# First batch in a fixed order, and another order of products and sums, in a spectral filter with a gated feed-forward block

## The chip, the core and the metric

The kernel runs on one core of one Trainium2 chip. The metric is the time on the device in microseconds (us), from the first instruction to the last, as the median of several runs. A profile is one execution taken by the hardware profiler; its times are counted from the start of that execution.

A core has a matrix engine (TensorE, PE in the profile; its weight loads have a row of their own, PEld), a vector engine (VectorE, DVE), an engine for functions of one operand (ScalarE, ACT), a general engine (GpSimd, POOL) and a queue engine (SyncE, SP). Each takes its own instructions in the order of the program and waits on semaphores for the others. TensorE writes to PSUM alone, where the kernel keeps one bank for the spectral part and seven for the rest. GpSimd does not read PSUM here.

## The reference, cut to what matters

```python
# x: 8 x 3008 x 256, filt_r and filt_i: 1505 x 256, w_gate and w_val: 256 x 1536, w_out: 1536 x 256
X = np.fft.rfft(x, axis=1)
Y = X * (filt_r + 1j * filt_i)[None, :, :]
y = np.fft.irfft(Y, n=x.shape[1], axis=1).astype(np.float32)
t = y.reshape(24064, 256)
g = t @ w_gate
silu = g * (1.0 / (1.0 + np.exp(-g)))
out = (silu * (t @ w_val) @ w_out).astype(np.float32)
```

The three weights arrive as 64-bit floats; the kernel reads each as two 32-bit words and rounds it on the chip.

## The kernel before

The transform of 3008 = 47 x 64 points runs in three stages of matmuls with tables: stage 1 (47 points) writes to a DRAM buffer d1, stage 2 reads it back transposed, multiplies by a table, by the filter and by a table again, and writes d2, stage 3 reads d2 and yields the sequence. Batch 0 passes stages 1 and 2 in a prologue; those of each later batch run beside the feed-forward products of the batch before it.

The feed-forward part works on chunks of 376 tokens, with a third of the hidden units at a time: 8 batches x 4 chunks x 3 thirds = 96 steps. The products are not plain block products: four blocks of tokens and weights are combined in sums and differences, so that 26 products P, Q, A, B, E (two matmuls each, for the gate and for the value) do the work of 32, and seven products W (six matmuls each) do that of eight in the second matmul. The order of everything in a step is one list of tokens. A token with a prime belongs to the step before:

```python
SCHEDULE = """
P3 x1.o' h23' g03' v12' Q0 x2.o' h03' Q2 x3.o' f0 x4.o' t0.0 x03 f2 x5.o' S01' x23 Q1 t0.1 P0 f1
P2 S00' c0 W1 s13 g0 t0.2 D01 c2 S11' y02 g2 h0 P1 o1 S10' Q3 c1 y01 A13 g1 x01 g3 S21' h1 e01
t1.0 y12 m13 s01 E01 S20' t1.1 A01 D02 W6 m01 t1.2 D12 l01 B13 u01 o6 B01 v01 g13 W7 S31' h13 g01
n3' t0.3 s02 h01 t2.0 S30' s12 t1.3 o7 A02 e13 t2.1 A12 h2 W4 m02 e23 m12 s03 E13 o4 E23 l13 B12
t2.2 u13 A03 g12 v13 t2.3 t3.0 e03 m03 h3 h12 B02 t3.1 E03 W5 g02 s23 l03 e02 h02 u03 A23 v03 t3.2
o5 E02 m23 t3.3 W2 l23 n2 l02 u23 v23 u02 t4.0 o2 e12 W3 v02 t4.1 E12 o3 B23 t4.2 l12 B03 x0.o
t4.3 n1 g23 u12
""".split()
BLOCKS = (3, 0, 2, 1)
```

P, Q, A, B, E are products; f, c, s, x, y, e, m, l prepare and combine their operands in PSUM; g, u are the gate's function, h, v the product with the value; D, S, n are sums of operands on GpSimd; W an output product, o its sum; t3.1 is the second slot for a piece of spectral work. What the tokens do:

```python
        def step(self, op):
            kind, at = op[0], op[1:]
            ij = [int(c) for c in at]
            i, j = ij[0], ij[-1]
            t, v, act = self.tiles, nc.vector, nc.scalar
            diagonal = len(ij) == 1
            if kind in "PQ":
                first = (kind == "P") == (i == 3)
                if first:
                    self.bank(f"k{i}")
                self.product(op, f"k{i}", first)
            elif kind == "f":
                pin(act.mul(self.small(f"f{i}", f"f{i}", 1), t[f"k{i}"], -1.0))
            elif kind == "D":
                pin(sub(nc.gpsimd, self.small(f"D{at}", "D", 2), t[f"f{i}"], t[f"f{j}"]))
            elif kind == "c":
                pin(act.copy(out=self.small(f"c{i}", f"c{i}", 1), in_=t[f"k{i}"]))
            elif kind == "x" or kind == "s" and at not in VIA_SBUF[0]:
                dst = self.small(f"x{at}", "x", 3) if kind == "x" else self.bank(f"a{at}")
                pin(v.scalar_tensor_tensor(
                    out=dst, in0=t[f"k{j}"], scalar=-1.0, in1=t[f"f{i}" if j == 3 else f"D{at}"],
                    op0=ALU.mult, op1=ALU.add))
            elif kind == "s":
                pin(act.copy(out=self.bank(f"a{at}"), in_=t[f"x{at}"]))
            elif kind == "y" or kind == "e" and at not in VIA_SBUF[1]:
                dst = self.small(f"y{at}", "y", 2) if kind == "y" else self.bank(f"e{at}")
                pin(negated_sum(dst, t[f"k{j}"], t[f"c{i}"]))
            elif kind == "e":
                pin(act.copy(out=self.bank(f"e{at}"), in_=t[f"y{at}"]))
            elif kind in "AB":
                self.product(op, f"a{at}", False)
            elif kind == "m":
                pin(act.copy(out=self.small(f"m{at}", "m", 3), in_=t[f"a{at}"]))
            elif kind == "E":
                self.product(op, f"e{at}", False)
            elif kind == "l":
                pin(sub(v, t[f"e{at}"], t[f"e{at}"], t[f"m{at}"]))
            elif kind in "gu":
                ps = t[f"k{i}" if diagonal else f"{'a' if kind == 'g' else 'e'}{at}"]
                pin(act.activation(out=self.small(op, "g", 3, 1)[:, 0], in_=ps[:, 1], func=AF.Silu))
            elif kind in "hv":
                ps = t[f"k{i}" if diagonal else f"{'a' if kind == 'h' else 'e'}{at}"]
                g = t[("g" if kind == "h" else "u") + at][:, 0]
                dst = self.place(i, j) if kind == "h" else self.place(j, i)
                pin(v.tensor_tensor(out=dst, in0=ps[:, 0], in1=g, op=ALU.mult))
            elif kind == "S":
                h = self.hs[j]
                dst, a, b, f = ((4, 1, 2, add), (7, 4, 0, sub), (5, 0, 1, sub), (6, 3, 7, sub))[i]
                pin(f(nc.gpsimd, h[:, dst], h[:, a], h[:, b]))
            elif kind == "n":
                if self.following:
                    combine_sequence(self.following(), i)
```

Rounding half a weight (36 such halves), and the combinations of one third's weights:

```python
    def round_half(i):
        # ... (raw words in raw; tiles pw and w from pools of two buffers)
        pin(v.tensor_scalar(out=man, in0=high, scalar1=0xFFFFF, scalar2=None,
                            op0=ALU.bitwise_and))
        pin(v.tensor_scalar(out=pw, in0=high, scalar1=20, scalar2=0x7FF,
                            op0=ALU.logical_shift_right, op1=ALU.bitwise_and))
        pin(nc.scalar.activation(out=w, in_=man, func=AF.Copy, scale=2.0 ** -20, bias=1.0))
        pin(nc.scalar.activation(out=pw, in_=pw, func=AF.Relu, bias=off_t))

        load_weights(i + NRAW - 1)
        yield
        pin(v.tensor_scalar(out=pw, in0=pw, scalar1=255.0, scalar2=2.0 ** 23,
                            op0=ALU.min, op1=ALU.mult))
        pin(v.scalar_tensor_tensor(out=pw.rearrange(flat), in0=raw.rearrange(flat2)[:, :, 1],
                                   scalar=0x80000000, in1=pw.rearrange(flat),
                                   op0=ALU.bitwise_and, op1=ALU.bitwise_or))
        pin(v.scalar_tensor_tensor(out=w.rearrange(flat), in0=raw.rearrange(flat2)[:, :, 0],
                                   scalar=2.0 ** -52, in1=w.rearrange(flat),
                                   op0=ALU.mult, op1=ALU.add))
        e = nc.gpsimd
        pf = pw.bitcast(FP32)
        if use == "proj":
            j, l = at
            dst = wo_t[:, j]
            pin(e.tensor_tensor(out=dst[:, ts(l, 2), :], in0=w, in1=pf, op=ALU.mult))
        # ... (four more sums for a w_out half; for a w_gate or w_val half two products and up to two sums, all on GpSimd)
    def round_next():

        i = rounding[0]
        rounding[0] += 1
        for h in halves[i:i + 1] + (halves[i - 1:i] if i else []):
            next(h, None)

    def combine_weights(g, i, j):

        d = j - i
        wt_f = weights_of(0, 0, g).rearrange("p s z f -> p s (z f)")
        m = wt_f[:, SLOT[f"A{i}{j}"]]
        ui, uj, yi, yj = [wt_f[:, SLOT[f"{p}{q}"]] for p in "PQ" for q in (i, j)]
        if d == 1:
            pin(negated_sum(m, ui, uj))
        else:
            pin(add(nc.vector, m, ui, uj))
            pin(nc.vector.tensor_scalar(out=m, in0=m, scalar1=-1.0 / d, scalar2=None, op0=ALU.mult))
        pin(sub(nc.vector, wt_f[:, SLOT[f"B{i}{j}"]], yi, m))
        pin(add(nc.gpsimd, wt_f[:, SLOT[f"E{i}{j}"]], yj, m))

    # when they run in batch 0: step -> token -> what follows it (r: one round_next)
    eight = {t: "r" for t in ("P3", "Q1", "P1", "E01", "W6", "W7", "A12", "E23")}
    pairs = {"E13": [(0, 3)], "B12": [(2, 3), (0, 2)], "E03": [(0, 1), (1, 2)], "A23": [(1, 3)],
             "B03": [0, 1, 2, 3]}
    PREPARE = {0: eight | pairs | {t: "r" for t in ("A01", "E02", "W3", "B23")},
               1: eight | pairs,
               2: {t: "r" for t in ("P3", "Q1", "P0", "P2")},
               3: {t: "r" for t in ("P3", "Q1", "P0", "P2")}}
```

Batch 0's prologue and the parts of it that the change touches:

```python
        def stage1(self, u):

            p1 = spool0 if self.b == 0 and u % 2 else t1pool
            t1 = p1.tile([NK, NV, C], FP32, name=f"t1_{self.b}_{u}", tag="t1", bufs=2)
            ps = self.bank(f"pa_{self.b}_{u}")
            self.pinned(nc.tensor.matmul(out=ps[0:NK], lhsT=wf_t, rhs=self.x.pop(u),
                                         start=True, stop=True))
            if self.b:
                self.load_x(u + 3)
            yield
            copy = nc.scalar.copy if self.b else nc.vector.tensor_copy
            self.pinned(copy(out=t1, in_=ps[0:NK]))
            queue = nc.scalar if self.b else nc.gpsimd
            self.pinned(queue.dma_start(out=self.d1_rows[:, ts(u, NV), :], in_=t1))
        # ... stage2a(u): two matmuls into ps, then
            lo, hi = slice(0, 64), slice(64, 128)
            v = nc.vector
            if self.b:
                fi = f[hi, 1]
                pin(v.tensor_tensor(out=pt, in0=ps, in1=f[:, 0], op=ALU.mult))
            else:
                fi = f[hi]
                for h in (lo, hi):
                    v.tensor_tensor(out=pt[h], in0=ps[h], in1=f[lo], op=ALU.mult)
            self.pinned(v.scalar_tensor_tensor(out=qt[lo], in0=ps[hi], scalar=-1.0, in1=fi,
                                               op0=ALU.mult, op1=ALU.mult))
            yield
            self.pinned(v.tensor_tensor(out=qt[hi], in0=ps[lo], in1=fi, op=ALU.mult))
            yield
            self.pinned(add(nc.gpsimd, pt, pt, qt))
        # ... stage2b(u): two matmuls of pt, a ScalarE copy to g, two stores to d2 from ScalarE's queue
        for i in range(4):
            spec.load_x(i)
        spec.load_tables()
        for i in range(NRAW - 1):
            load_weights(i)
        nc.sync.dma_start(out=wi_t, in_=wi_dram.ap())
        def run(piece):
            for _ in piece:
                pass

        for u in range(N_ONE):
            run(spec.stage1(u))
        for _ in range(4):
            round_next()
        lag = 3
        for u in range(N_TWO + lag):
            if u < N_TWO:
                run(spec.stage2a(u))
            if u >= lag:
                run(spec.stage2b(u - lag))
    for i in range(2):
        spec.load_t4(0, i)
    following = Spectral(1)
    for u in range(3):
        following.load_x(u)
    for _ in range(5):
        round_next()
    for i, j in PAIRS:
        combine_weights(0, i, j)
    warm()
    for step in range(4):
        run(spec.stage3(0, step))
    for d in (2, 3, 1):
        combine_sequence(spec.y[0], d)
```

At the end the list is passed once more for the last step's output products, and then its o tokens with a prime: the last sums, and six stores on GpSimd's queue.

## Time and profile before

| | us |
|---|---|
| median of 3 runs | 3137.53 (3137.41 to 3138.02) |
| span of the profiled execution | 3139.4 |
| TensorE busy | 2989.7 (95%) |
| TensorE weight loads busy | 2831.6 (90%) |
| VectorE busy | 1974.2 (63%) |
| GpSimd busy | 1585.3 (50%) |
| ScalarE busy | 1513.4 (48%) |
| mean granted TensorE clock | 0.982 |

The page of a profile has one row per engine in 40 equal slices, each digit being the busy share in tenths, and a row with the clock that the throttle granted to TensorE. A view by stretches gives the same for any cuts, in microseconds. The timeline prints merged instructions in order of time; what stands in brackets behind one is the idle time of its engine before it and who ended it ("0.92 <-ACT we L634": 0.92 us, ended by ScalarE's instruction of line 634 that writes tile we). The table of waits sums these. A line number of the kernel names a group of instructions: L268 to L282 are the rounding, L453, L479, L504 and L525 the matmuls of stages 1, 2 (twice) and 3, L603 the products and L679 the output products. A tile's name is the program's own: wk, wa and we are the banks of the P and Q, A and B, and E products. An fp32 matmul is recorded as two instructions of TensorE.

### The profile page before, as it was taken

What the parts mean: (1) busy time and instruction counts of PE and PEld (TensorE: products, weight loads), DVE (VectorE), ACT (ScalarE), POOL (GpSimd) and SP (SyncE); (2) the same over time, 40 slices, a digit from 0 to 9 for tenths busy, and PEclk for the clock granted to TensorE, in tenths of its full rate; (3) what the DMA queues carried; (4) which work ended last, traced back from release to release, by engine and by line L of the source; (5) the groups of instructions that cost most, each with busy time, mean ns of one, the idle gap of its engine ahead of it and who ended that gap; (6) DMA issues with size and microseconds to landing.
All of it is one profiled execution on the core that took longest, in us unless ns stands there. A gap on an engine that the chain in (4) does not pass through costs nothing.

```text
span 3139.4 us, 57065 instructions
## 1 busy us (share of the span) xinstructions
PE 2989.7 (95%) x20124; PEld 2831.6 (90%) x20124; DVE 1974.2 (63%) x4446; ACT 1513.4 (48%) x3898; POOL 1585.3 (50%) x1778
## 2 busy tenths in 40 slices
PE   5578999999999999999999999999999999999997
PEld 2467999999999999999999999999999999999997
DVE  4576666557665666656665576656666566666664
ACT  1344445554455544554455545555445544455542
POOL 2555545455554556445454555445554545555543
PEclk9778999999999999999999999999999999999998
DMA  8435655557655556456554566555664565544441
GB/s 238 142 126 175 210 184 176 176 177 224 185 165 174 191 187 201 159 174 203 189 183 163 186 211 191 161 179 187 203 195 154 179 200 182 188 148 141 141 133 51
DMA packets 210503, 551.72 MB, mean 176 GB/s; under 512 B 32502, under 2 KB 105462, under 8 KB 209362
## 3 DMA queue, kind: packets, MB, share of 16 engines
q1 hardware_dynamic: 150572, 462.06, 46.3%
q10 hardware_dynamic: 49408, 58.22, 6.4%
q0 software_dynamic: 10240, 27.80, 2.5%
q8 instruction: 161, 2.64, 0.3%
q14 instruction: 122, 1.00, 0.1%
HBM read 462.76 MB, written 85.20 MB: 175 GB/s over the span
## 4 chain that ended last, share of the span: by engine, by line
PE 80%; ACT 5%; DVE 3%; POOL 2%; issue 1%; DMA 1%; ACTq 1%; POOLq 0%; DVEq 0%
PE wa L603 21%; PE wA L679 14%; PE wk L603 13%; PE we L603 11%; PE wG L679 8%; PE wF L679 4%; PE pd L525 3%; PE pa L453 3%; PE pc L504 2%; PE pb L479 2%; DVE y L218 1%; ACT g L645 1%; ACT c L622 1%; ACTq L513 1%; DMA out_dram<-o 1%
## 5 line engine op out<-in xcount | busy, mean ns | idle before, releaser
L603 PE MATMUL wa<-y_t,wt_t 128*128 128x188 f32 x4560 | 867.1, 327 | 12.2 <-POOL w L302 5.3
L603 PEld LDWEIGHTS wa<-y_t,wt_t 128*128 128x128 f32 x4560 | 739.8, 191 | 53.7 <-issue 19.3
L679 PE MATMUL wA<-wo_t,h 128*128 128x128 f32 x4608 | 587.5, 278 | 17.4 <-POOL wo_t L290 11.2
L679 PEld LDWEIGHTS wA<-wo_t,h 128*128 128x128 f32 x4608 | 569.3, 194 | 24.1 <-POOL wo_t L290 11.6
L214 POOL TENSOR_TENSOR h<-h 128x376 f32<-128x376 f32 x576 | 552.5, 984 | 0.0
L603 PE MATMUL wk<-y,wt_t 128*128 128x188 f32 x3040 | 536.0, 325 | 14.5 <-ACT f L618 14.5
L214 DVE TENSOR_TENSOR we<-we,m 128x376 f32<-128x376 f32 x576 | 311.3, 556 | 375.8 <-ACT m L638 177.1
L603 PEld LDWEIGHTS wk<-y,wt_t 128*128 128x128 f32 x3040 | 494.4, 192 | 31.6 <-ACT f L618 15.4
L603 PE MATMUL we<-y_t,wt_t 128*128 128x188 f32 x2280 | 454.4, 328 | 32.2 <-ACT we L634 29.0
L603 PEld LDWEIGHTS we<-y_t,wt_t 128*128 128x128 f32 x2280 | 366.3, 191 | 71.2 <-ACT we L634 37.1
L638 ACT COPY m<-wa 128x376 f32<-128x376 f32 x576 | 270.3, 476 | 280.5 <-PE wa L603 246.1
L211 POOL TENSOR_TENSOR h<-h 128x376 f32<-128x376 f32 x192 | 185.0, 987 | 430.2 <-DVE h L650 429.7
L645 ACT ACTIVATE g<-wa 128x188 f32<-128x188 f32 x576 | 188.6, 328 | 425.6 <-PE wa L603 267.4
L214 POOL TENSOR_TENSOR D<-f,f 128x376 f32<-128x376 f32 x288 | 280.3, 987 | 72.2 <-ACT f L618 72.1
L645 ACT ACTIVATE u<-we 128x188 f32<-128x188 f32 x576 | 185.0, 326 | 247.6 <-DVE we L214 239.2
L679 PEld LDWEIGHTS wG<-wo_t,h 128*128 128x128 f32 x2304 | 283.9, 193 | 12.5 <-issue 10.7
L679 PE MATMUL wG<-wo_t,h 128*128 128x128 f32 x2304 | 291.3, 277 | 0.0
L211 POOL TENSOR_TENSOR lent<-lent 128x512 f32<-128x512 f32 (+2 forms) x94 | 116.2, 1237 | 326.3 <-DVE lent L495 304.8
L668 POOL DMA_DIRECT2D out_dram<-o x192 | 110.8, 582 | 315.5 <-DVE o L211 313.4
L650 DVE TENSOR_TENSOR h<-wa,g 128x188 f32<-128x188 f32 x576 | 201.6, 350 | 83.9 <-ACT g L645 79.0
L650 DVE TENSOR_TENSOR h<-we,u 128x188 f32<-128x188 f32 x576 | 201.7, 350 | 78.2 <-ACT u L645 68.3
L218 DVE SCALAR_TENSOR_TENSOR y<-wk,c 128x376 f32<-128x376 f32 x288 | 157.2, 546 | 99.6 <-ACT c L622 98.3
(108 smaller groups left out, 3777.2 us busy)
## 6 DMA issues: line engine op xcount, KB each, us to landing
wt_t<-w_all SPq DMA_DIRECT2D x186, 896.0 KB
wt_t<-w_all SPq DMA_DIRECT2D x186, 768.0 KB
t<-d SPq DMA_DIRECT2D x64, 384.0 KB
lent<-d SPq DMA_DIRECT2D x180, 128.0 KB
d<-lent ACTq DMA_DIRECT2D x180, 128.0 KB
d<-t ACTq DMA_DIRECT2D x112, 192.0 KB
lent<-de_tbl SPq DMA_DIRECT2D x84, 256.0 KB
lent<-in_filt_r_dram SPq DMA_DIRECT2D x336, 64.0 KB
```

Of the source, the lines that this page charges most:

```text
L211: return eng.tensor_tensor(out=dst, in0=a, in1=b, op=ALU.add)
L214: return eng.tensor_tensor(out=dst, in0=a, in1=b, op=ALU.subtract)
L218: return nc.vector.scalar_tensor_tensor(out=dst, in0=a, scalar=-1.0, in1=b, op0=ALU.mult, op1=ALU.subtract)
L453: self.pinned(nc.tensor.matmul(out=ps[0:NK], lhsT=wf_t, rhs=self.x.pop(u), start=True, stop=True))
L479: self.pinned(nc.tensor.matmul(out=ps[:, i, :], lhsT=self.tb[u][:, i, 0, :], rhs=t2[:, i, :], start=True, stop=True))
L525: self.pinned(nc.tensor.matmul(out=psv[:, n, :], lhsT=self.t4[k, i][:, n, ts(cb, 128)], rhs=wi_t, start=True, stop=True))
L603: pin(nc.tensor.matmul(out=ps[:, z], lhsT=self.wt[:, SLOT[p], z], rhs=rhs, start=start and z == 0, stop=True, skip_group_check=True))
L638: pin(act.copy(out=self.small(f"m{at}", "m", 3), in_=t[f"a{at}"]))
L645: pin(act.activation(out=self.small(op, "g", 3, 1)[:, 0], in_=ps[:, 1], func=AF.Silu))
L650: pin(v.tensor_tensor(out=dst, in0=ps[:, 0], in1=g, op=ALU.mult))
L668: pin(nc.gpsimd.dma_start(out=rows[(TOK[t] + skip) // NH:(TOK[t] + 128) // NH, ts(2 * k + i, NH), :], in_=outs[b, k][i][skip:128, t, :]))
L679: pin(nc.tensor.matmul(out=self.tiles[at][:, t, :], lhsT=self.hs[i][:, HID[p], t0:t0 + 128], rhs=wo_t[:, JB * q + i, WO[p], :], start=star ...
```

## The change

It has five parts.

1. Batch 0's prologue is pinned to the order in which the program is written (later batches were already). Eight half weights are loaded in it ahead of the last third of the stage tables, into the room of that third, and their rounding and the first third's combinations run before stage 2; eight further rounding calls run before stage 3. What is left for batch 0's steps is spread anew. Stage 1's copies move from VectorE to ScalarE.
2. In batch 0's stage 2, one product of 128 partitions takes the place of two of 64; ScalarE copies the filter's real part to both halves for it. The d2 stores move from ScalarE's queue to SyncE's and GpSimd's, and stage 3's first results use the seven banks. The warming matmuls before stage 3 become 28, of which the 14 new ones have 512 columns.
3. The list of tokens has another order; the blocks' order changes with it, the tiles of y and m get one buffer more, those of h lose one of eight parts, since the sum S2 overwrites an operand.
4. In the weights' combinations the B part moves from VectorE to GpSimd.
5. At the end the sums S are split over VectorE and GpSimd, the output products of the last step run in an order of their own, and its stores go out on three queues.

The diff, cut to its core:

```diff
 SCHEDULE = """
-P3 x1.o' h23' g03' v12' Q0 x2.o' h03' Q2 x3.o' f0 x4.o' t0.0 x03 f2 x5.o' S01' x23 Q1 t0.1 P0 f1
-P2 S00' c0 W1 s13 g0 t0.2 D01 c2 S11' y02 g2 h0 P1 o1 S10' Q3 c1 y01 A13 g1 x01 g3 S21' h1 e01
-t1.0 y12 m13 s01 E01 S20' t1.1 A01 D02 W6 m01 t1.2 D12 l01 B13 u01 o6 B01 v01 g13 W7 S31' h13 g01
-n3' t0.3 s02 h01 t2.0 S30' s12 t1.3 o7 A02 e13 t2.1 A12 h2 W4 m02 e23 m12 s03 E13 o4 E23 l13 B12
-t2.2 u13 A03 g12 v13 t2.3 t3.0 e03 m03 h3 h12 B02 t3.1 E03 W5 g02 s23 l03 e02 h02 u03 A23 v03 t3.2
-o5 E02 m23 t3.3 W2 l23 n2 l02 u23 v23 u02 t4.0 o2 e12 W3 v02 t4.1 E12 o3 B23 t4.2 l12 B03 x0.o
-t4.3 n1 g23 u12
+Q0 o3' t4.2' W2 f0 S00' S01' x0.o' t0.0 x1.o' Q1 t0.1 x2.o' P3 x3.o' f1 t4.3' W1 x4.o' S10' x03 S11'
+s13 x5.o' P1 o1 t0.2 P0 o2 c1 D01 A13 g1 c0 S20' Q2 S21' g0 y01 m13 t1.0 h0 f2 s01 W6 t1.1 h1 x23
+D02 P2 o6 D12 A01 c2 B13 g2 n3' m01 t0.3 S30' t1.2 x02 W7 S31' g13 y12 y02 B01 h13 o7 t1.3 t2.0 s02
+s12 g01 h2 Q3 t2.1 h01 e12 A02 y23 W4 e02 y03 m02 g3 A12 o4 t2.2 E12 m12 B02 t2.3 l12 E02 u12 e13
+g02 t3.0 h3 s23 l02 B12 v12 E13 t3.1 h02 u02 A23 n2 l13 g12 v02 W5 s03 e23 h12 e01 m23 A03 o5 u13
+E23 t3.2 m03 v13 E01 l23 e03 t3.3 t4.0 l01 u23 B23 v23 u01 t4.1 E03 n1 v01 g23 B03 l03 W3 h23 g03
+u03 h03 v03
 """.split()
 KS = (-1, 0, 1, 2)
-BLOCKS = (3, 0, 2, 1)
+
+LAST = "W1 o1 W2 o2 W6 o6 W5 o5 W3 o3 x0.o x1.o x2.o W7 o7 W4 o4 x3.o x4.o x5.o".split()
+BLOCKS = (0, 1, 3, 2)
 # ...
-        pin(sub(nc.vector, wt_f[:, SLOT[f"B{i}{j}"]], yi, m))
+        pin(sub(nc.gpsimd, wt_f[:, SLOT[f"B{i}{j}"]], yi, m))
 # ...
-    eight = ...   # (the old PREPARE, as above)
+    PREPARE = {(0, "B03"): [("k", 1, p) for p in range(4)], (1, "B03"): [("k", 2, 0)],
+               (2, "A01"): [("k", 2, p) for p in (1, 2, 3)]}
+    for step, tokens in ((0, "Q0 P3 P0 Q2 A01 B01"), (1, "Q0 P3 P1 A13 P2 B13 Q3 A12 B02 B12"),
+                         (2, "A13 P2 B01 A02")):
+        for token in tokens.split():
+            PREPARE.setdefault((step, token), []).append("r")
+    for g, pairs in ((1, "0Q313 0A0201 0A1202 0B0212 0B1223 0A2303"),
+                     (2, "1A0213 1E1201 1E0202 2Q112 2P123 2Q203")):
+        for p in pairs.split():
+            PREPARE.setdefault((int(p[0]), p[1:-2]), []).insert(0, ("c", g, int(p[-2]), int(p[-1])))
 # ...
-        for n in (TQ, 2 * TQ):
+        for n in (512, 512, TQ, 2 * TQ):
 # ...
-            copy = nc.scalar.copy if self.b else nc.vector.tensor_copy
-            self.pinned(copy(out=t1, in_=ps[0:NK]))
+            pin(nc.scalar.copy(out=t1, in_=ps[0:NK]))
 # ...
-            if self.b:
-                fi = f[hi, 1]
-                pin(v.tensor_tensor(out=pt, in0=ps, in1=f[:, 0], op=ALU.mult))
-            else:
-                fi = f[hi]
-                for h in (lo, hi):
-                    v.tensor_tensor(out=pt[h], in0=ps[h], in1=f[lo], op=ALU.mult)
-            self.pinned(v.scalar_tensor_tensor(out=qt[lo], in0=ps[hi], scalar=-1.0, in1=fi,
-                                               op0=ALU.mult, op1=ALU.mult))
+            fr, fi = (f[:, 0], f[hi, 1]) if self.b else (self.real.pop(u), f[hi])
+            pin(v.tensor_tensor(out=pt, in0=ps, in1=fr, op=ALU.mult))
 # ...
+        def real_part(self, u):
+
+            if u < N_TWO:
+                self.real[u] = early("fr", u)
+                for h in (slice(0, 64), slice(64, 128)):
+                    pin(nc.scalar.copy(out=self.real[u][h], in_=self.f[u][0:64]))
 # ...
+                queue = nc.scalar if self.b else (nc.sync, nc.gpsimd)[p]
 # ...
-                dst, a, b, f = ((4, 1, 2, add), (7, 4, 0, sub), (5, 0, 1, sub), (6, 3, 7, sub))[i]
-                pin(f(nc.gpsimd, h[:, dst], h[:, a], h[:, b]))
+                dst, a, b, f = ((4, 1, 2, add), (6, 4, 0, sub), (1, 0, 1, sub), (5, 3, 6, sub))[i]
+                pin(f(eng or nc.gpsimd, h[:, dst], h[:, a], h[:, b]))
 # ...
+                    queue = (nc.sync, nc.scalar, nc.gpsimd)[t] if last else nc.gpsimd
 # ...
+        for i, n in enumerate((0, 2, 2, 4)):
             spec.load_x(i)
-        spec.load_tables()
-        for i in range(NRAW - 1):
 # ...
+            if u in (7, 8, 10, 11, 13, 14, 15):
+                round_next()
+        for _ in range(2):
             round_next()
+        for u in range(3):
+            spec.load_two(u)
+        spec.load_tables(2)
+        for i, j in PAIRS:
+            combine_weights(0, i, j)
+        for u in range(3):
+            spec.real_part(u)
 # ...
+    warm()
+    for _ in range(8):
         round_next()
-    for i, j in PAIRS:
-        combine_weights(0, i, j)
-    warm()
     for step in range(4):
         run(spec.stage3(0, step))
-    for d in (2, 3, 1):
-        combine_sequence(spec.y[0], d)
+    for d in (2, 1, 3):
+        combine_sequence(spec.y[0], d, nc.vector if d == 1 else nc.gpsimd)
 # ...
+                        g0.step(op, nc.vector if ghost and op[0] == "S" and op[2] == "1" else None)
 # ...
-    for token in SCHEDULE:
-        if token.endswith("'") and (token[0] == "o" or ".o" in token):
-            older.project(token.rstrip("'"))
+    for op in LAST:
+        older.project(op, True)
```

## The prediction

> **What bounds the kernel now.** I read the page first. Part 1 has TensorE busy for 95% of the span; part 2 shows where it is not:
>
> ```profile
> PE   5578999999999999999999999999999999999997
> PEclk9778999999999999999999999999999999999998
> ```
>
> From the fifth slice on (one slice is 78 us) TensorE is full and its clock is full. The loss lies in the first four slices and the last. So I cut the trace into stretches: start to the end of the first stage's matmuls (37 us), the wait behind it (to 56.2), the second stage (to 95.7), warming and third stage (to 115), then four work steps of batch 0, from one first wk product to the next; then one step far inside, and the tail. The columns are length, then busy us (and instructions) of each engine, granted clock, DMA share and GB/s:
>
> ```profile
> 37.00:56.20 19.20, 0.03 (x1) 0.06 (x1) 8.04 (x21) 3.34 (x8) 7.25 (x15) 1.00 0.78 236
> 56.20:95.70 39.50, 27.48 (x97) 19.68 (x98) 35.58 (x53) 6.45 (x11) 15.83 (x14) 0.96 0.54 143
> 95.70:115.00 19.30, 14.32 (x61) 11.99 (x60) 9.31 (x26) 7.82 (x18) 7.45 (x15) 0.77 0.70 197
> 115.00:181.10 66.10, 34.57 (x129) 30.47 (x128) 40.67 (x113) 24.69 (x59) 36.96 (x53) 0.68 0.49 168
> 181.10:235.10 54.00, 39.87 (x211) 36.64 (x211) 41.98 (x103) 24.22 (x62) 29.29 (x46) 0.81 0.26 81
> 235.10:275.30 40.20, 33.81 (x200) 30.70 (x199) 23.05 (x60) 19.20 (x50) 21.89 (x28) 0.87 0.64 220
> 275.30:313.60 38.30, 32.89 (x201) 29.78 (x200) 25.53 (x60) 17.90 (x48) 21.38 (x30) 0.91 0.41 132
> 2852.40:2879.60 27.20, 26.28 (x190) 25.89 (x189) 17.78 (x41) 13.70 (x39) 18.04 (x19) 1.00 0.38 125
> 3103.10:3139.40 36.30, 19.04 (x122) 18.10 (x120) 8.08 (x17) 2.02 (x7) 11.00 (x14) 0.73 0.07 21
> ```
>
> The reader is to see: work steps 0 to 3 take 66.1, 54.0, 40.2 and 38.3 us; later ones 27.2 to 31. In steps 0 and 1 VectorE carries 41 to 42 us, over twice the 17.8 us of a plain step, because the weights' rounding runs there. TensorE waits for it at 0.68 of its clock. In the second stage VectorE is busy 35.6 of 39.5 us: it is the bound there.
>
> Inside, the matmuls come at a fixed pace. The timeline shows 0.64 us for one product (two matmuls) and 1.34 us for one output product (six). A plain step has 26 products and 7 output products: 26 x 0.64 + 7 x 1.34 = 26.0 us. It takes 27.2, so 1.2 us is bubble. Most is one wait, once a step:
>
> ```profile
> 2865.18 0.87 PE L603 MATMUL we<-y_t,wt_t 128*128 128x188 f32 x4 [0.92 <-ACT we L634]
> ```
>
> E01 waits for ScalarE's copy into its bank. In batch 1 (368.4 us between equal places of two batches) 7.4 us are bubble: 12 steps of 26.0 make 312, the spectral matmuls at their median start-to-start paces (32 x 0.433, 96 x 0.216, 128 x 0.112 us) 49; so 0.62 us a step on the mean.
>
> **What the Trainium skill says.** "TensorE: Matmul & The Clock Gate", What's actually happening: an idle window of about 3.4 us halves the clock, a busy one restores it. The trace agrees in steps 0 to 3 (0.68 to 0.91), but not wholly: the first stage's 94x512 matmuls pass at 0.85 us for half a product, and at 0.43 later, though TensorE is busy throughout. "SBUF — State Buffer", Who interferes with whom: a VectorE instruction with two SBUF inputs shares a read interface with GpSimd. It fits that the 128x256 subtractions of the weights take 0.41 us at best and 0.96 at most. "DMA: Bandwidth & Descriptors", Issuing engines are not separate DMA queues: more queues save only issue time; no run here isolates that yet, and I count the three store queues so.
>
> **The change, part by part.**
>
> 1. *Up to the second stage.* Eight half weights are loaded and nine rounding calls run while VectorE was nearly idle (8.0 of the 19.2 us, 8.3 of the first 37). One call costs VectorE 0.28 + 0.28 + 0.28 + 0.42 + 0.41 = 1.7 us at the shortest durations, ScalarE 0.40 + 0.49, GpSimd about 3 x 0.455. A third of the tables (2 MB) loads after the second stage's first data rather than before; two MB of weights come in earlier. The wait at 37 to 56 ran at 236 GB/s with the queue full, so bytes decide it: I count about 1 MB less ahead, 4 us, and start the second stage at 52.
>
> 2. *Second stage.* The two 64-partition products by the real filter (0.69 us each) become one of 128 (0.68); ScalarE copies make its operand. VectorE per unit: 0.68 + 0.69 + 0.68 = 2.06 us for 2.75; the units came every 2.85 us and should come every 2.1. ScalarE gets 0.59 + two 64x512 copies, some 0.5 each by the 0.59 of its 128x512 copy; GpSimd 1.26 + a store's issue of 0.53. All are under 2.1. But the weights' combinations (12 GpSimd sums of 0.84) stand before GpSimd's first sum, to about 58 us; I add 3. VectorE ends at 52 + 3 + 25 = 80, against 92.3.
>
> 3. *To the first product.* Eight rounding calls now stand between, for five. Calls follow one another at the pace of the loop VectorE, ScalarE, VectorE, GpSimd, for the tiles w and pw have two buffers: before, the L268 operations began at 96.5, 101.4, 106.0, 108.5, so 4.0 apart with a wait for loads among them. I take 3.5: 28 us, to 108; the third stage's copies and sums add 4. First product at 112 (before: 115.0). The warming matmuls grow from 8.5 us to about 20 by their columns (a row of 512 is 0.43 us at full clock, twice for a product), hidden in those 28.
>
> 4. *Steps 0 to 3.* They keep 20 rounding calls out of 28: six, ten, four, none, for twelve, eight, four, four. The B combinations go to GpSimd, so a combination costs VectorE 0.4 to 0.7 us. Step 0: plain VectorE work without output sums 17.8 - 7 x 0.55 = 14 us, 6 x 1.7 = 10, combinations 3.4, third stage 1, together 28, and 9 of waits in the in-order queue, half of what it had (66.1 - 40.7 = 25): 37. Step 1: 17.8 + 17 + 2 + 1 = 38, and 5: 43. Step 2: 17.8 + 6.8 + 2 = 27, under TensorE's own 30.5: 33. Step 3: 30.5. Sum 143.5 against 198.6, so 55 us, and 3 from the earlier beginning: **58 us**.
>
> 5. *Inside.* In the new order E01 stands third from last among the E products, some 15 us after its operand is made; the first E, E12, has one output product and A12 (2.0 us) behind its last producer. By the same prefix sums the tightest pair is A23 behind its copy s23, some 0.5 us. I take a quarter of a us off each of about 92 steps: **23 us**, out of the 57 (0.62 each) that are there.
>
> 6. *The end.* Last products end at 3107.9. GpSimd's eight sums run to 3115.6 and hold TensorE; six stores are issued at 3127.1 for 3.45 us, on one queue. Now the sums are split over two engines: 4 x (0.98 + 0.55) = 6.1 us if they exclude each other, under the first three output products. Seven output products are 9.4 us, the last sum 0.8, one issue 0.6; behind its last issue GpSimd's queue took 8 us to close, and I keep that. About 21 from the last product for 31.5: **10 us**.
>
> Sum 58 + 23 + 10 = 91; I take 87 for what in-order queues add that I don't see, so 3050.
>
> **Rivals.** (a) *A new wait in the ordered start.* Stores of the first stage stand behind GpSimd's rounding, ScalarE's copies behind rounding halves that wait for VectorE; if a call costs 4 us there, stage one ends 10 us later and the rounding is not hidden. For it: the 3.5 us loop. Against: 19 us of idle follow anyway. It would make 3070. (b) *DMA becomes the bound in the second stage*: 512 KB a unit in 2.1 us is 250 GB/s, plus 2 MB of tables, against 271 reached in the first 37 us. Then units stay at 2.6 and 6 us are lost: 3056. (c) *The new order brings as many bubbles as it removes*: VectorE's share rises to about 0.8 where a second stage runs beside products, and an in-order queue delays a copy. Then nothing comes from part 5: 3073. (d) *All bubbles vanish and step 1 stays near TensorE's pace*: 3010.
>
> **Range and chances.** (a) and (c) together give 3093, (d) 3010. The 2% line is at about 3075; only a failure of part 4 by half or two rivals at once reaches it. Faster by over 2%: 0.77; within 2%: 0.20; slower: 0.03, if the new order costs over 1.5 us in each step.
>
> **What would show it.** Right: L268 instructions from the first 25 us; second-stage units every 2.1 us; first wk near 112; steps 0 to 3 of about 37, 43, 33, 31 us with VectorE over 0.8 busy in the first two; plain steps of 26.5 to 27.0 with no 0.9 us wait of E01; last store issued some 13 us after the last product. Wrong: GpSimd idle behind VectorE in the first stage with a later second stage, plain steps at 27.2 or more, or a new releaser above 10 us in the table of waits inside.

## The result, and the profile after

The changed kernel takes **3044.4 us** (3043.3 to 3047.2), the kernel before 3137.5 us in the same series: a ratio of 0.9706, 95% interval 0.9689 to 0.9723. Predicted were 3050. The total is right, but two of its three terms are not: the start gave little more than half of what was counted, and the inside more than twice as much.

First the two rows of the page of the kernel after that answer to those shown of before, TensorE's busy share and its clock in 40 slices of 76 us:

```profile
PE   5779999999999999999999999999999999999998
PEclk9889999999999999999999999999999999999999
```

One slice fewer is short of full: TensorE is full from the fourth on. Then its table by stretches, cut at the same places of the program as before: the wait ahead of the second stage (from 37 us in both), the second stage, the calls and the third stage, steps 0 to 3, a plain step, and the end from the last F output product. That product stands elsewhere in the new order, so the ends are compared in the second table and not by these last rows. Columns: stretch, length, busy us (instructions) of TensorE, weight loads, VectorE, ScalarE, GpSimd, then clock, DMA share, GB/s.

```profile
37.00:55.50 18.50, 0.01 (x1) 0.04 (x1) 11.15 (x27) 8.64 (x18) 12.99 (x25) 1.00 0.75 199
55.50:92.00 36.50, 26.08 (x93) 20.15 (x94) 28.82 (x43) 17.56 (x29) 25.05 (x28) 0.86 0.73 196
92.00:121.10 29.10, 23.14 (x92) 14.41 (x91) 11.81 (x39) 7.93 (x18) 12.74 (x28) 0.93 0.86 259
121.10:162.60 41.50, 30.52 (x126) 26.26 (x127) 35.45 (x76) 23.40 (x58) 27.56 (x39) 0.76 0.44 141
162.60:212.50 49.90, 38.71 (x212) 34.86 (x211) 40.45 (x97) 26.02 (x66) 30.21 (x48) 0.83 0.34 108
212.50:249.10 36.60, 32.72 (x200) 29.08 (x200) 30.08 (x63) 18.92 (x49) 28.61 (x36) 0.95 0.73 242
249.10:279.40 30.30, 30.30 (x201) 27.76 (x200) 17.34 (x41) 16.26 (x43) 12.24 (x15) 1.00 0.51 161
2859.30:2885.20 25.90, 25.90 (x190) 25.90 (x189) 17.20 (x42) 13.41 (x38) 12.22 (x16) 1.00 0.41 132
3019.20:3043.30 24.10, 8.93 (x74) 8.22 (x72) 7.43 (x10) 0.00 (x0) 4.44 (x5) 0.84 0.11 33
```

The first wk product comes at 121.1 us, later than before (115.0). Steps 0 to 3 take 41.5, 49.9, 36.6 and 30.3 us; in the first two VectorE is busy 0.85 and 0.81 of the time. The plain step is 25.90 us with TensorE busy for 25.90 of them: no bubble is left in it. From this come the three terms (before minus after, in the two profiles):

| part | before | after | gained | predicted |
|---|---|---|---|---|
| to the start of step 4 | 313.6 | 279.4 | 34.2 | 58 |
| start of step 4 to start of step 95 (91 steps) | 2766.9 | 2712.5 | 54.4 | 23 |
| start of step 95 to the end | 58.9 | 51.4 | 7.5 | 10 |
| span | 3139.4 | 3043.3 | 96.1 | 91 |

The expectations below have 55 and 6.7 us for the second and third gain, from a start of step 95 in the kernel before that was read 0.8 us late.

### The profile page after: what moved, and what is told of

Read it like the earlier page. It is cut to its first block, busy times and chain, and to the rows that moved or that the text cites. A ratio compares the mean times of both kernels' runs of the same rounds, so it can differ in the third digit from the quotient of the medians.

```text
span 3043.3 us, 57524 instructions
## 1 busy us (share of the span) xinstructions
PE 2948.7 (97%) x20152; PEld 2827.3 (93%) x20152; DVE 1923.5 (63%) x4407; ACT 1581.1 (52%) x4130; POOL 1599.7 (53%) x1797
## 4 chain that ended last, share of the span: by engine, by line
PE 89%; ACT 1%; issue 1%; DMA 1%; DVE 1%; POOL 1%; ACTq 0%; POOLq 0%; DVEq 0%
PE wa L600 23%; PE wA L677 16%; PE wk L600 15%; PE we L600 12%; PE wG L677 8%; PE wF L677 4%; PE pd L522 3%; PE pa L459 3%; PE pb L476 2%; PE pc L503 2%; DMA out_dram<-o 1%; ACTq L511 0%; ACT lent L507 0%; POOL h L213 0%; ACT y_t L561 0%
## 5 line engine op out<-in xcount | busy, mean ns | idle before, releaser
L600 PE MATMUL wa<-y_t,wt_t 128*128 128x188 f32 x4560 | 902.5, 324 | 7.4 <-ACT wa L626 4.7
L600 PEld LDWEIGHTS wa<-y_t,wt_t 128*128 128x128 f32 x4560 | 749.0, 191 | 34.1 <-issue 15.8
L600 PE MATMUL wk<-y,wt_t 128*128 128x188 f32 x3040 | 586.2, 326 | 17.4 <-ACT f L615 11.4
L677 PEld LDWEIGHTS wA<-wo_t,h 128*128 128x128 f32 x4608 | 564.2, 192 | 24.3 <-issue 14.4
L600 PEld LDWEIGHTS wk<-y,wt_t 128*128 128x128 f32 x3040 | 493.2, 192 | 49.9 <-issue 22.6
L600 PE MATMUL we<-y_t,wt_t 128*128 128x188 f32 x2280 | 441.4, 323 | 0.0
L600 PEld LDWEIGHTS we<-y_t,wt_t 128*128 128x128 f32 x2280 | 377.1, 190 | 1.3 <-DVE we L220 0.7
L220 DVE SCALAR_TENSOR_TENSOR y<-wk,c 128x376 f32<-128x376 f32 x480 | 244.5, 542 | 153.6 <-ACT we L631 104.3
L615 ACT ACTIVATE f<-wk 128x376 f32<-128x376 f32 x288 | 139.9, 486 | 253.9 <-PE wk L600 214.3
L622 DVE SCALAR_TENSOR_TENSOR x<-wk,f 128x376 f32<-128x376 f32 x192 | 104.5, 544 | 237.4 <-PE wk L600 236.5
L619 ACT COPY c<-wk 128x376 f32<-128x376 f32 x288 | 136.3, 473 | 223.7 <-PE wk L600 222.1
L631 ACT COPY we<-y 128x376 f32<-128x376 f32 x480 | 223.5, 487 | 50.6 <-issue 28.2
```

Source lines behind the costliest of these rows:

```text
L220: return nc.vector.scalar_tensor_tensor(out=dst, in0=a, scalar=-1.0, in1=b, op0=ALU.mult, op1=ALU.subtract)
L600: pin(nc.tensor.matmul(out=ps[:, z], lhsT=self.wt[:, SLOT[p], z], rhs=rhs, start=start and z == 0, stop=True, skip_group_check=True))
L622: pin(v.scalar_tensor_tensor(out=dst, in0=t[f"k{j}"], scalar=-1.0, in1=t[f"f{i}" if j == 3 else f"D{at}"], op0=ALU.mult, op1=ALU.add))
L677: pin(nc.tensor.matmul(out=self.tiles[at][:, t, :], lhsT=self.hs[i][:, HID[p], t0:t0 + 128], rhs=wo_t[:, JB * q + i, WO[p], :], start=star ...
```

## The experiments

A difference between two of the ratios below carries some 0.0023 (7 us) of uncertainty, and the second stage begins anywhere from 52.6 to 56.7 us in nine profiles of kernels that are alike up to there. Edits at the start are therefore judged by the stretch they touch, and the total only where it moves by more. All edits are of the changed kernel.

### Does the order alone make the inside?

**Old order.** The SCHEDULE text of the kernel before put back, all else kept:

```diff
-Q0 o3' t4.2' W2 f0 S00' S01' x0.o' t0.0 ... u03 h03 v03
+P3 x1.o' h23' g03' v12' Q0 x2.o' h03' Q2 ... t4.3 n1 g23 u12
```

> The changed kernel with the old order of products and sums and nothing else undone. Theory (the order alone removes the bubbles inside): the inside part of the gain, 0.61 us a step over 91 steps = 55 us, goes away again: about 3099 us (3088 to 3110), plain steps near 27.2 us instead of 25.9, and the E01 wait for ScalarE's copy, about 0.9 us a step, is back at the top of the waits of TensorE. Rival (the extra tiles, a third y and a fourth m, carry it): at most 15 us slower, 3059 or less, and plain steps below 26.3.

Measured: 3102.6 us, ratio 0.9880 (0.9865 to 0.9895), so 0.0174 x 3138 = 55 us slower than the change. Its steps 4 to 94 take 2760.0 us, 47.5 more than the 2712.5 of the change; 4.8 of the rest lie at the start, 3.9 at the end. A plain step, first by stretch, then the wait in it (start, duration, what it is, idle before it and its releaser):

```profile
2873.40:2900.60 27.20, 26.37 (x190) 25.89 (x190) 17.82 (x41) 12.77 (x35) 11.47 (x12) 1.00 0.50 156
```
```profile
2886.02 0.90 PE L600 MATMUL we<-y_t,wt_t 128*128 128x188 f32 x4 [0.83 <-ACT we L631]
```

The step is back at 27.20 us and the E01 wait with it. So the order carries most of the 54.4 us inside. With the old order, the extra y and m tiles are worth no more than the 6.9 us that stay of 54.4. The new order can't do without them: a kernel with two y and three m tiles in the new order, expected to be 10 to 35 us slower, deadlocks and has no time. It is likely, but not shown, that operations then wait for tiles that only later ones in the same queues free.

**One product moved.** E01 stands directly behind W5, where, in the one step that I had read, ScalarE's copy for it is done 0.5 us too late:

```diff
-... W5 s03 e23 h12 e01 m23 A03 o5 u13 E23 t3.2 m03 v13 E01 l23 ...
+... W5 s03 e23 h12 e01 E01 m23 A03 o5 u13 E23 t3.2 m03 v13 l23 ...
```

> The changed kernel with one product moved: E01 stands directly behind the output product W5, ahead of A03, where ScalarE's copy into its bank (about 2854.0 in the step read, against 2853.5 for the end of W5) is just not done. Theory (a wait of TensorE inside is lost one for one, and the gain inside is the slack of a few such pairs): a wait of 0.5 to 0.7 us at E01 in each of 96 steps, so 45 to 65 us slower, 3089 to 3109. Rival (a bubble at one place is made up at others because later operands have more slack, or PE runs at its own pace): under 15 us slower.

Measured: 3078.3 us, ratio 0.9806 (0.9791 to 0.9820): 31 us slower by ratio. The waits of TensorE from 400 to 2900 us (total, times, longest), this kernel first, then the change:

```profile
PE we L600 <- ACT we L631: 24.2, 34, 2.1
PE wk L600 <- ACT f L615: 0.8, 3, 0.3
```
```profile
PE wa L600 <- ACT wa L626: 4.7, 8, 1.2
PE wk L600 <- ACT f L615: 2.0, 4, 0.8
PE wA L677 <- ACT o L689: 1.9, 4, 0.9
PE pb L476 <- DMA lent<-d: 0.7, 1, 0.7
```

A wait at one product is lost at the end: 24.2 us of listed waits and 31 at the end. But it came 34 times, not in each of 96 steps, so the 31 us lie between the theory's 45 to 65 and the rival's 15. I had read the slack off one step; in part of the plain steps ScalarE is ahead and nothing is lost (26.0 us, others take 26.6; 25.9 in the change). A slack has to be read in the loaded steps as well.

### Why did the start give 34 us and not 58?

**The tables.** The fourth unit of the second stage waits for its data, which stands behind the 2 MB of tables. Here they are issued behind the third unit instead:

```diff
-        spec.load_tables(2)
         for i, j in PAIRS:
             combine_weights(0, i, j)
 # ...
                 run(spec.stage2a(u))
+                if u == 2:
+                    spec.load_tables(2)
```

> The changed kernel with the last third of the tables (2 MB) loaded behind the third unit of the second stage instead of ahead of it. Theory (the 7.3 us for which the fourth unit waited are these 2 MB standing ahead of its data in the queues): the wait goes below 2 us, the second stage's VectorE work ends 5 to 8 us earlier than 90.3, the first wk product comes 4 to 8 us before 121.1, and the end follows: 3036 to 3041. Rival (the rounding behind waits for its own loads or another pace takes the gain): the second stage ends earlier but the first product moves by under 2 us, 3042 to 3046.

Measured: 3041.2 us, ratio 0.9689 (0.9674 to 0.9703). The wait in the timeline, the change first, then this kernel:

```profile
67.39 2.04 PE L476 MATMUL wpb<-room,tb 128*128 128x256 f32 x4 [7.33 <-DMA room<-d]
```
```profile
73.01 2.04 PE L476 MATMUL wpb<-room,tb 128*128 128x256 f32 x4 [4.77 <-DMA room<-d]
```

It moved from the fourth unit to the seventh and shrank. From the first to the last product by the filter's real part this stage takes 27.5 us, for 29.0 to 30.5 in profiles with the tables ahead: 1.5 us at the least. The tables do make the wait, but issuing them later mostly hands it to later units. The first wk product comes only 1.8 us earlier, as the rival had it, though not for the rival's reason; the total moved within its uncertainty.

**The raw weights.** Of the eight calls ahead of the third stage three waited for raw data: 1.8, 3.0 and 3.1 us. Here the six halves not yet loaded go ahead at once:

```diff
+    with tc.tile_pool(name="mid", bufs=1) as mid:
+        for i in range(11, 17):
+            raws[i] = mid.tile([128, 2, 128, 2], U32, name=f"raw_{i}", tag=f"raw{i}")
+            pin(nc.sync.dma_start(out=raws[i], in_=weights[i][0]))
         # the third stage's loads, batch 1's x, warm() and the eight calls follow
```

> The changed kernel with the raw weights of the eight calls ahead of the third stage loaded at once, ahead of the third stage's loads and batch 1's x, into tiles of their own, instead of two calls ahead in three tiles. Theory (a call took 3.9 us rather than 3.5 or its loop's 3.07 because VectorE waited 8.0 us for raw loads): these waits go below 2 us, the eight calls take 25 us rather than 30.3, the first wk product comes 4 to 6 us before 121.1, and the end follows: 3037 to 3041. Rival (the transfers as a whole are the bound there, so the wait turns up at the third stage's loads, or in step 0): 3042 to 3046.

Measured: 3045.1 us, ratio 0.9701 (0.9685 to 0.9717). Among the eight calls one wait for raw data (2.7 us) is left, and the first wk product comes at 115.9 us, 27.1 us behind the first of the eight calls for 30.8. But step 0 takes 44.1 us for 41.5, and the total does not show a gain. Half of what was won ahead of step 0 was gone at its end, since the wait for raw data turned up there, as the rival said. VectorE is not busier in this step 0 (34.9 us for 35.5), but it stands still once as it never does in the change:

```profile
131.91 0.29 DVE L276 TENSOR_SCALAR w<-raw 128x256 uint32<-128x256 uint32 x1 [3.19 <-DMA raw<-in_moe_w_out_dram]
```

An earlier start by itself is not given back: with the tables late and with the end undone (below), step 0 begins 1.8 and 4.0 us earlier than in the change, and steps 0 to 2 take 41.5, 49.9 and 36.6 us in all three.

**Five calls for eight.** Three of the calls moved into step 0:

```diff
-    for _ in range(8):
+    for _ in range(5):
         round_next()
-    (0, "Q0 P3 P0 Q2 A01 B01")
+    (0, "Q0 Q1 P3 P0 A13 Q2 P2 A01 B01")
```

> The changed kernel with five rounding calls ahead of the third stage and nine in step 0, for eight and six. Theory (ahead of the third stage a call costs 3.9 us of waiting for its loop, in step 0 it costs VectorE's 2.5 us): the first wk product comes some 11 us earlier, near 110, step 0 grows by 7 to 9 us to about 50, and the end comes 2 to 5 us earlier, 3039 to 3042. Rival (in step 0 each call costs as much as it saves, VectorE being the bound there at 35.5 of 41.5 us and slowed by GpSimd): 3043 to 3048.

Measured: 3046.2 us, ratio 0.9707 (0.9692 to 0.9721). The rival holds. By stretch, steps 0 and 1:

```profile
113.80:162.90 49.10, 28.38 (x128) 25.66 (x128) 39.66 (x91) 25.01 (x63) 32.77 (x49) 0.76 0.42 137
162.90:212.60 49.70, 35.77 (x213) 32.51 (x212) 40.47 (x97) 25.99 (x66) 30.25 (x48) 0.93 0.35 114
```

The first product comes 7.3 us earlier than 121.1, step 0 ends at 162.9 where it ended at 162.6. It fits that what counts up to there is how much VectorE still has to do, and not when TensorE may begin.

**ScalarE out of the way.** In steps 0 to 3 ScalarE stands 19.8 us behind the first of VectorE's bit operations, 15.8 of them in steps 0 and 1. Here its two operations of a call are issued three to four tokens later:

```diff
-        pin(nc.scalar.activation(out=w, in_=man, func=AF.Copy, scale=2.0 ** -20, bias=1.0))
+        yield      # what follows is issued DELAY = 3 tokens later
+        pin(nc.scalar.activation(out=w, in_=man, func=AF.Copy, scale=2.0 ** -20, bias=1.0))
```

> The changed kernel with the two ScalarE operations of each rounding call in steps 0 to 2 issued three to four tokens of the schedule later, so that ScalarE's queue does not stand for VectorE's bit operations. Theory (steps 0 and 1 are long because ScalarE stands 19.8 us behind VectorE's rounding, which delays its copies f, which TensorE waits 14.7 us for): steps 0 and 1 together shorten by 8 to 14 us of 91.4, 3030 to 3037. Rival (VectorE's own work, 35.5 of 41.5 and 40.5 of 49.9 us busy, sets these steps): under 4 us, 3040 to 3044.

Measured: 3046.6 us, ratio 0.9703 (0.9687 to 0.9720); steps 0 and 1 take 39.8 and 50.4 us, 90.2 for 91.4. ScalarE's place in the queue was not the cause.

**One VectorE operation less.** The limit at 255 is left out, and the factor 2^23 goes into ScalarE's operation:

```diff
-        pin(nc.scalar.activation(out=pw, in_=pw, func=AF.Relu, bias=off_t))
+        pin(nc.scalar.activation(out=pw, in_=pw, func=AF.Relu, scale=2.0 ** 23, bias=off_t))
 # ... off_t holds -896 x 2^23
-        pin(v.tensor_scalar(out=pw, in0=pw, scalar1=255.0, scalar2=2.0 ** 23,
-                            op0=ALU.min, op1=ALU.mult))
```

> The changed kernel with one of the five VectorE operations of each rounding call (the limit at 255 and the shift by 2^23) taken into ScalarE's operation ahead of it, as its scale; the limit, which matters only for weights above the range of fp32, is left out. Theory (VectorE's own work is the bound of steps 0 and 1, whatever comes ahead of them): 16 calls less 0.39 to 0.46 us each in steps 0 and 1, so these two steps together 5 to 8 us shorter than 91.4, and 3035 to 3040 at the end. Rival (the order in the queues and the waits for GpSimd and ScalarE set them): under 3 us, 3041 to 3046.

Measured: 3042.0 us, ratio 0.9692 (0.9675 to 0.9708). Steps 0, 1 and 2:

```profile
121.00:161.20 40.20, 28.94 (x127) 24.95 (x128) 33.28 (x71) 23.27 (x58) 27.60 (x39) 0.78 0.43 138
161.20:207.90 46.70, 37.83 (x212) 33.78 (x211) 37.61 (x87) 26.03 (x66) 30.54 (x48) 0.85 0.37 113
207.90:243.30 35.40, 32.37 (x200) 29.16 (x199) 28.28 (x59) 18.97 (x49) 28.62 (x36) 0.95 0.76 249
```

VectorE is busy 2.2 and 2.8 us less in steps 0 and 1, and these are 1.3 and 3.2 us shorter, step 2 another 1.2. That is just under the range of the theory, but nearly all that VectorE lost came through: its idle time in steps 0 and 1 stays, 16.0 us for 15.5. Such differences are clear of the 0.1 us to which these steps repeat, while the total's is not clear of its uncertainty. This is the edit that shows VectorE's work as the bound there. Its operations were longer than I had counted; the groups of VectorE in step 1 of the change (busy us, mean ns | idle before):

```profile
L276 DVE TENSOR_SCALAR w<-raw 128x256 uint32<-128x256 uint32 x10 | 6.1, 605 | 3.3 <-POOL wt_t L213 1.7 <-POOL wt_t L310 1.0 <-POOL wo_t L298 0.6
L278 DVE TENSOR_SCALAR pw<-raw 128x256 uint32<-128x256 uint32 x10 | 6.0, 600 | 0.0
L290 DVE SCALAR_TENSOR_TENSOR w<-raw,w 128x256 f32<-128x256 uint32 x10 | 4.4, 443 | 0.0
L287 DVE SCALAR_TENSOR_TENSOR pw<-raw,pw 128x256 uint32<-128x256 uint32 x10 | 4.4, 439 | 0.3
L285 DVE TENSOR_SCALAR pw<-pw 128x256 uint32<-128x256 uint32 x10 | 3.9, 386 | 0.0
```

They sum to 2.47 us a call, for the 1.7 of the shortest durations. Where no GpSimd operation overlaps, L278 takes 0.28 to 0.29 us in every one of 17 cases; the long ones look like this (VectorE, then GpSimd, on the timeline of step 0):

```profile
142.00 1.07 DVE L278 TENSOR_SCALAR pw<-raw 128x256 uint32<-128x256 uint32 x1
142.99 1.07 DVE L285 TENSOR_SCALAR pw<-pw 128x256 uint32<-128x256 uint32 x1
```
```profile
141.89 2.02 POOL L216 TENSOR_TENSOR D<-f,f 128x376 f32<-128x376 f32 x2
```

Each of the two begins beside one of GpSimd's two differences and ends just behind it.

**The two engines by themselves.** A kernel that computes nothing of the reference times three VectorE operations 16 times alone and 16 times beside sums of GpSimd:

> A kernel that computes nothing of the reference: it times three VectorE operations, 16 times each alone and then 16 times beside sums of GpSimd of two 128x376 tiles (0.98 us each): the shift of 128x256 raw words, the scalar_tensor_tensor of two 128x256 tiles, and a 128x376 subtraction with one input in PSUM. Theory (VectorE and GpSimd exclude each other for operands in SBUF): alone about 0.28, 0.42 and 0.55 us; beside GpSimd the first two take over 0.8 us on the mean, or GpSimd's sums lengthen by as much; the one with a PSUM input is within 10% of its time alone. Rival (the lengthening in steps 0 and 1 comes of something else, such as transfers or semaphores): all three within 10%.

The groups of 16 on VectorE's timeline, alone and beside GpSimd in turn, and then GpSimd's sums beside the first operation, beside the second, and alone:

```profile
6.31 5.20 DVE L42 TENSOR_SCALAR pw<-raw 128x256 uint32<-128x256 uint32 x16
13.52 16.86 DVE L42 TENSOR_SCALAR pw<-raw 128x256 uint32<-128x256 uint32 x16
32.40 7.32 DVE L46 SCALAR_TENSOR_TENSOR w<-raw,w 128x256 f32<-128x256 uint32 x16
41.80 17.93 DVE L46 SCALAR_TENSOR_TENSOR w<-raw,w 128x256 f32<-128x256 uint32 x16
61.75 9.29 DVE L50 TENSOR_TENSOR c<-psum,c 128x376 f32<-128x376 f32 x16
73.12 9.30 DVE L50 TENSOR_TENSOR c<-psum,c 128x376 f32<-128x376 f32 x16
```
```profile
13.10 17.14 POOL L54 TENSOR_TENSOR h<-h,h 128x376 f32<-128x376 f32 x16
41.38 18.07 POOL L54 TENSOR_TENSOR h<-h,h 128x376 f32<-128x376 f32 x16
91.55 17.14 POOL L54 TENSOR_TENSOR h<-h,h 128x376 f32<-128x376 f32 x16
```

Beside GpSimd VectorE gets in one operation for each sum, whether it needs 0.33 or 0.46 us; GpSimd's sums lose nothing beside the shift and 0.9 us beside the two-input operation (18.07 for 17.14); and an operation with one input in PSUM is not touched. The theory holds for these operations, and the long shifts of the calls look the same. What it costs the steps is a matter of the next run.

**Calls where GpSimd is quiet.** Nine of the ten calls of step 1 moved behind the S sums and D differences:

```diff
-    (1, "Q0 P3 P1 A13 P2 B13 Q3 A12 B02 B12")
+    (1, "P3 B13 B01 Q3 A02 A12 B02 B12 E13 A23")
-    "1A0213 1E1201 1E0202 ..."
+    "1E0213 1E1201 1E1302 ..."
```

> The changed kernel with nine of the ten rounding calls of step 1 moved behind the S sums and D differences of GpSimd, into the second half of the step, and three combinations of weights moved accordingly. Theory (a rounding operation on VectorE that starts beside a sum of GpSimd waits for its end, 0.28 us becoming 1.05 to 1.10 us): the mean of the two bit operations falls from 0.60 to below 0.45 us, step 1 shortens by 3 to 6 us of 49.9, 3038 to 3042. Rival (what counts is VectorE's place in the order: calls bunched in the second half delay the e and l operations there, or the output products of step 2 wait for their weights): step 1 and 2 together no shorter, 3043 to 3050.

Measured: 3046.0 us, ratio 0.9704 (0.9689 to 0.9719). The edit did not bring the quiet that it was meant to: L276 and L278 still take 0.57 us on the mean, since the first of the moved calls still meet the last S sums and D differences (GpSimd's queue runs late there), and the later ones the sums of the weights' combinations; and step 1 takes 52.8 us for 49.9. TensorE waits there 7.3 us for ScalarE's copies into the a banks and 3.9 for VectorE's e, which now stand behind the bunched calls. So the rival holds for this order, and what the steps would take without the exclusion is not shown by any run.

### The end

The eight last sums all on GpSimd and the six stores on one queue, with the new order of the last products kept:

```diff
-        g0.step(op, nc.vector if ghost and op[0] == "S" and op[2] == "1" else None)
+        g0.step(op, None)
-        queue = (nc.sync, nc.scalar, nc.gpsimd)[t] if last else nc.gpsimd
+        queue = nc.gpsimd
```

> The changed kernel with the end undone: the eight last sums all on GpSimd and the last six stores all on GpSimd's queue, the new order of the last products kept. Theory (sums on two engines and stores on three queues are the 6.7 us that the end is shorter): 4 to 8 us slower than 3044, 3048 to 3052, and TensorE waits for GpSimd's sums again at the end. Rival (the new order of the last products, which puts the sums of the first halves ahead, is what shortens the end): under 2 us slower, 3043 to 3046.

Measured: 3040.7 us, ratio 0.9691 (0.9677 to 0.9706), not slower. TensorE's first wait among the last output products, the change first, then this kernel:

```profile
3023.45 1.58 PE L677 MATMUL wA<-wo_t,h 128*128 128x128 f32 x12 [2.75 <-DVE o L213]
```
```profile
3016.15 1.38 PE L677 MATMUL wA<-wo_t,h 128*128 128x128 f32 x10 [0.46 <-POOL h L216]
```

In the change VectorE's queue has three of the sums and then the output sum that frees the bank:

```profile
3019.10 3.74 DVE L216 TENSOR_TENSOR h<-h 128x376 f32<-128x376 f32 x3
3022.76 0.54 DVE L213 TENSOR_TENSOR o<-o,wA 128x384 f32<-128x384 f32 x1
```

The three take 1.25 us each, beside GpSimd's half of the sums, where the first alone took 0.54. So dividing them gains little, and the output sum comes late. From the last F product to the last matmul's end the change takes 13.1 us and this kernel 10.95; from there to the end 11.0 and 12.45. So three store queues save 1.45 us and the divided sums cost 2.1; the joined kernels below, with the sums on GpSimd and three queues, have the best of both, 10.95 and 11.0. From its last product to the end this kernel takes 25.9 us, for 31.5 before and 26.6 in the change, so the new order of the last products saves 5.6 there, by subtraction: no run takes it back alone. Ahead of the last product the change saves 2.6 us more of step 95 (24.8 for 27.4), and these are the token list's: the kernel with the old order has 27.4 again.

In other executions the wait of 2.75 us costs more. The kernel with the tables late has the same end:

```profile
3018.78 2.05 PE L677 MATMUL wA<-wo_t,h 128*128 128x128 f32 x12 [2.73 <-DVE o L213]
3020.62 2.71 PE L677 MATMUL wG<-wo_t,h 128*128 128x128 f32 x12
```

These two products take 1.58 and 1.50 us in the change; the granted clock is 0.72 from 3018 to 3022 us here, and 1.00 in the change over its last products. Of eight kernels with the new list and this end, five are like this one, with 17.0 to 17.2 us from the last product to the last matmul, and three like the change with 15.6. With the wait at 0.46 or 0.47 us, in three kernels, no product is slow. In the kernel before, three output products that follow the wait of 2.67 us take 2.7 to 2.9 us each, at a granted clock of 0.50: some 4 us of its long end.

### What helps, joined

The tables behind the third unit, the raw weights at once, one VectorE operation less, and the last sums on GpSimd with three store queues; the second kernel also has the B combinations back on VectorE:

```diff
-        pin(sub(nc.gpsimd, wt_f[:, SLOT[f"B{i}{j}"]], yi, m))
+        pin(sub(nc.vector, wt_f[:, SLOT[f"B{i}{j}"]], yi, m))
```

> Four edits joined: the last third of the tables behind the third unit of the second stage, the raw weights of the eight calls loaded at once, one VectorE operation less in each rounding call (the limit at 255 left out), and the eight last sums all on GpSimd while the last stores stay on three queues. From the runs before: 1.8 us in the second stage, some 4 us ahead of the third stage of which steps 0 and 1 gave back half, 4.5 to 5.7 us in steps 0 to 2, some 2 us at the end. Theory (VectorE bounds the steps 0 to 2, so gains ahead of them add up only in part): 7 to 11 us faster, 3033 to 3038, a ratio of 0.9665 to 0.9685. Rival (gains from the single edits add up to nothing more than the best of them, since each only moves a wait): 3040 to 3044.

> The same four edits, and besides the B combinations of the weights back on VectorE from GpSimd, as in the kernel before. Theory (a sum on GpSimd keeps VectorE out for its whole 0.75 to 0.82 us, so a 0.41 us sum taken off VectorE relieves nothing while both are busy): within 2 us of the four joined edits or up to 4 us faster. Rival (work taken off VectorE is work off the path): 3 to 6 us slower, 18 sums of 0.41 to 0.9 us in steps 0 to 2 and the second stage.

Measured: **3029.7 us**, ratio 0.9659 (0.9646 to 0.9672), and 3033.1 us, ratio 0.9662 (0.9649 to 0.9675). With four edits joined the kernel is 0.0047 x 3138 = 15 us faster than the change, with some 7 us of uncertainty: more than any single edit, so the rival falls, and the total does not exclude the 7 to 11 us expected. From the calls to the end of step 1, and the end:

```profile
87.00:110.80 23.80, 23.18 (x93) 14.45 (x93) 9.77 (x31) 7.97 (x19) 12.67 (x28) 1.00 0.69 187
110.80:151.90 41.10, 27.03 (x126) 23.40 (x127) 32.71 (x70) 23.19 (x58) 27.76 (x40) 0.83 0.63 221
151.90:199.20 47.30, 36.96 (x212) 33.07 (x211) 37.92 (x87) 26.08 (x66) 30.51 (x48) 0.89 0.34 114
3004.00:3026.00 22.00, 9.11 (x74) 8.32 (x72) 3.88 (x7) 0.00 (x0) 7.14 (x9) 0.84 0.12 36
```

Step 4 begins 15.0 us earlier (264.4), and the end is 2.1 us shorter. VectorE's part of the second stage is 3.2 us shorter, the stretch from there to the first product 5.4, steps 0 to 2 together 4.7, and 1.5 is scatter of the beginning (54.0 us for 55.5). So the gains of the single edits add nearly in full. Step 0 takes 0.9 us more than with less work on VectorE alone; VectorE waits 2.1 us in it for raw data.

What the B combinations do is left open by the total: 0.0003 in the ratio, with 0.0018 of uncertainty. By stretches, in one profile of each, the second kernel is the slower: steps 0 to 2 take 44.6, 47.9 and 34.3 us, 126.8 for 123.4. In its step 0 VectorE is busy 34.2 us for 32.8, though GpSimd is busy only 24.3 for 27.8. That speaks for the rival, 3 to 6 us slower, and against the theory that work taken off VectorE in this way relieves nothing.

## Why the total was right and its terms were not

The sum 91 met 96 by luck: one term was over-sized by 24 us and another under-sized by 31. By the prediction's own steps:

1. *Up to the second stage*: 52 predicted, 55.5 in this profile, 52.6 to 56.7 over nine. The step that failed is that bytes decide it: in the stretch from 37 us the bytes fell as counted, from 4.5 to 3.7 MB (236 GB/s x 19.2 us, 199 x 18.5), and the stage began only 0.7 us earlier. The last store of d1 had landed at 46.1 us (before: 47.5), but SyncE issued the first read-back of d1 at 51.4 (49.6): its queue had stood 4.3 us at the load ahead of it, until raw weights had landed (1.2 before). Why that load waits for them is open.
2. *Second stage*: the pace is right, 2.16 us a unit for 2.1. The step that failed is the end at 80, a sum without any wait for data: it was 90.3, 3.5 from the later start and 6.5 from two waits (5.2 and 1.3 on VectorE) for the units' data. Rival (b) had the cause, transfers, but as a slower pace; it is a standstill where 2 MB stand ahead.
3. *To the first product*: 28 + 4 = 32 us counted from the end of VectorE's second stage, 30.8 measured. Right; 121.1 instead of 112 is all inherited.
4. *Steps 0 to 3*: 143.5 predicted, 158.3 measured. The mis-sized term is a rounding call on VectorE: **2.56 and 2.47 us in steps 0 and 1, not 1.7**. I had summed the shortest durations, though the trace of before has 1.90 and 2.30 us a call in its steps 0 and 1, and though the page "SBUF — State Buffer" of the Trainium skill, Who interferes with whom, which I quoted, calls the shared port an exclusive lock. The run of the two engines shows just that, with 5.20 against 16.86 us, and its PSUM case (9.29 and 9.30) agrees with the same section. The call's lengthening is 6 x 0.86 + 10 x 0.77 = 12.9 us, the combinations took 5.3 for 3.4 in step 0, and 3.7 us of y sums that the change gives VectorE there were not counted at all; the rest of VectorE's work was less than I took. So VectorE is busy 7.5, 2.5 and 3.1 us more than counted in steps 0 to 2. The waits were taken wrongly too: 9 us in step 0, called half of 25, which is not 9, and 6.0 measured; 5 in step 1 and 9.4 measured.
5. *Inside*: the mechanism is right, the order, and the size off: 0.60 us a step, not 0.25. I took a quarter of a us where the working itself had 0.62 of bubble and slack at every pair I examined. A plain step has 26.0 us of matmuls and takes 25.9. Rival (c) is refuted. Rival (d) is half right: the bubbles went, but step 1 did not come near TensorE's pace.
6. *The end*: 7.5 for 10, with 2.6 of it ahead of the last product, in the step itself. From the last product it takes 26.6 us, not 21: an eighth output product (1.34 us) follows it in the new order, and three waits for VectorE's sums (2.75, 0.74, 0.65) stand between. The terms that the working lists add to 18.8, not 21, and the closing behind the last issue, taken as 8 us, is 8.9 in the trace of before and 9.5 here. The last issue came 16.5 us behind the last product, for 13. The page "DMA: Bandwidth & Descriptors" of the Trainium skill, Issuing engines are not separate DMA queues, says that more queues save issue time only. The trace agrees in the main: behind the last matmul the end is 1.45 us shorter with three queues than with one, and 1.1 of that is issue time (1.72 us for three stores in a row on one queue, 0.59 for one).

Rival (a), a new wait in the ordered start, was not seen as put: the nine early calls ended before the second stage began, and the first stage's last store was issued at 42.7 us, for 43.8 before.

## What to carry to other kernels

When an in-order engine is the bound of a stretch, count its operations at the durations they have beside the other engines' work, not at their shortest, and add every operation that the change gives it. When loads are moved to win time ahead of such a stretch, look in it for the loads that now come later: here a wait of 3.2 us for raw weights in step 0 took back half of what the earlier loads had won, while mere earlier starts of 1.8 and 4.0 us were kept whole. And when an order is built so that operands are ready ahead, expect the whole bubble to go, and read the slack in the loaded steps, not in one plain one.

## What the hardware showed that I had not expected

VectorE and GpSimd do not slow each other in proportion: a run of VectorE's shifts, 0.33 us each alone, advances beside GpSimd's sums by one shift per sum, one every 1.05 us, while 16 sums take 17.14 us with them or without. The two-input operation gets in once per sum as well, and the sums take 18.07 us. At the end of the kernel both engines lose: VectorE's sums take 1.25 us for 0.54, and the three of GpSimd beside them 1.29 for 0.98. The single-input shift of 32-bit words is caught like the two-input operation; of the three tried, only the operation with an input in PSUM is free.
